# Infini-attention block with a gated FFN: sums evicted from PSUM bank by bank, full-width transposes, and a newly planned order

## Chip, cores and metric

The kernel runs on one core of a Trainium2 chip. The metric is the device time of one execution in microseconds (us). Engines are named as in the profile: PE (TensorE), DVE (VectorE), ACT (ScalarE), POOL (GpSimd), SP (the queue that issues most DMAs).

## What is computed

The input is 2048 tokens of width 448 in bfloat16. A layer norm with scale and shift from a condition vector `c` comes first, then attention with a compressive memory, then a second modulated layer norm and a gated FFN. The core of the reference:

```python
for s in range(4):                       # segments of 512 tokens, 16 heads of 28
    logits = einsum('bhqd,bhkd->bhqk', qs, ks) * scale + mask
    a_dot = softmax(logits) @ vs
    pq = phi(qs)                         # phi(t) = t + 1 if t > 0 else exp(t)
    a_mem = (pq @ M) / (pq . z + 1e-06)
    outs.append(g * a_mem + (1 - g) * a_dot)
    M = M + phi(ks)^T @ vs;  z = z + sum(phi(ks))
x = x + ga * (concat(outs) @ wo)
h = layernorm(x) * (1 + cb) + sb
x = x + gb * ((sigmoid(h @ w_gate) * (h @ w_up)) @ w_down)
```

The six vectors `sa, ca, ga, sb, cb, gb` are `silu(c) @ w_mod`; `q, k, v` come from the first modulated layer norm; the FFN's inner width is 1792.

## The kernel before

The work is cut into four segments of 512 tokens. For each segment the kernel does a layer norm (`ln1`), turns the tokens over so that features lie on partitions (`hT`), projects q, k and v (`proj`), computes logits, exps and attention sums for four groups of four heads (`attention`, `unit`), updates the memory (`memory`), does the output projection and second layer norm (`wo_ln2`), and the FFN in 14 chunks of 128 inner features (`ffn`).

Nothing is issued in the order of these loops. Every piece of work is a node of a graph (`Graph.add`) with a duration, the engines that may do it, its inputs, the ring slots it takes and the slots it uses. When all nodes are made, `Graph.run` plays the graph through on planned clocks: at each moment, an engine that is free takes the ready node with the highest rank (longest path to the end) plus priority. The priorities are the tables `PRM`, one entry a node. `STAY` is a bonus for a PE node in the same array mode as the one before it. Where two engines may do a node, `COST` weighs their planned durations against each other. The order found is the order in which the instructions are issued on each engine, SP's loads included; the durations in the code have no other effect. A slot is given back when the plan says that its last user has ended.

All matmul results lie in one PSUM tile `ps` of eight banks; a node takes banks by number as they are free, and any two free banks may make a pair. Transposes also write to PSUM.

The places that the change touches:

- `proj` (lines 891 to 923). A job of 14 matmuls at line 903 makes the k sums and the q sums of four heads in two banks. One eviction (`evac`, line 886 on ACT or line 888 on DVE) reads both banks with one access, whose step is the distance of the banks, and writes k and q with one access into the joint tile `kq_t`, in which the slots of k come first and those of q after them. The v sums of two token tiles (line 916) leave in the same way into two neighbouring tiles of `vt`. Planned durations are 840 and 1130 ns (ACT, DVE) for k and q, and 760 and 1010 for v.
- `pf2`, `lesser`, `greater` make the access on two banks:

```python
i, j = lesser(a, b), greater(a, b)
return ps[:, i:j + 1:j - i, :]
```

- `turned_once` (line 777) turns one token tile over in four transposes (line 782) for the second layer norm of every segment and the first layer norm of the last one. The tile `xn` has 512 columns, of which the last 64 are zeros, set once (line 585). The fourth transpose reads only 64 columns.
- `turned` (line 831) does the same for the other first layer norms with eight transposes a tile, at line 841, two of which are 64 wide. Each of the two then modulates the result into `hT` on DVE or ACT (lines 861, 863 and 797, 795).
- `memory` (line 940): transposes of k (line 950), exps, matmuls of the memory (line 969).
- Other lines that are named below: 1011 logits, 1025 and 1031 exps, 1041 and 1038 masks, 1070 attention sums, 1140 output projection, 1162 FFN gate and up, 1181 FFN down, 622 and 635 layer norm.

Of the kernel before, what the change touches and what calls it, by code (L numbers as in the profile page):

```python
# [7 lines left out]
BF16 = mybir.dt.bfloat16  # L8
# [43 lines left out]
    "mask": (3126070, 2037934, 2803786, 3505785, 3188009, 2852632, 3303572, 3533526, 3992806, 2545585, 2629448,  # L52
# [16 lines left out]
    "mem": (-123901, -236157, 540966, -358460, -167904, 74719, 3507, 330720, 598584, 648670, 613158, -673453, -487145,  # L69
# [18 lines left out]
    "tanh": (1212395, 1541798, 840180, 1390091, 2102771, 1519654, 1567471, 1153766, 1921369, 2277244, 2695092,  # L88
# [17 lines left out]
        -778556, -813758, 65300, -841338, -1381324, -626743, -443000, -615156, -409610, -941217, -462304, -867816,  # L106
        -636982, -465394, 452513, -909815, -380427, -10400),
}
STAY = 145391
COST = {"ACT": 0.829, "DVE": 0.85, "POOL": 0.804}  # L110


# [1127 lines left out]
```

## Time and profile before

| | |
|---|---|
| three runs, median (lowest, highest) | 268.8 us (268.68, 271.85) |
| profiled execution, time | 269.32 us |
| profiled execution, span | 267.6 us |
| busy PE, DVE, ACT, POOL | 248.3, 194.3, 162.2, 31.3 us |
| moved by DMA | 15.58 MB |

The span goes from the first to the last instruction in the profile, and the time has 1.7 us around it. Busy time is the union of an engine's instructions; a matmul's end is modelled, and matmuls overlap, so that the mean length of one (377 ns) is longer than the distance to the next. A row of the timeline or of the groups names the engine, the line of the kernel, what is written and read, and the count; a bracket or the part behind the bar tells how long the engine stood idle before it and which instruction ended that.

### The profile page before, as it was taken

The page shows a single profiled execution, that of the slowest core. Times are in us where ns is not written, and L with a number is a line of the kernel's source. Part 1 is how long each engine was busy: PE and PEld are TensorE (multiplying, and loading weights), DVE is VectorE, ACT ScalarE, POOL GpSimd, SP SyncE. Part 2 cuts the span into 40 slices and gives each one's busy share as a digit, 9 for nine tenths or more (in the row PEclk, how much of TensorE's full clock was granted, in tenths as well). Part 3 has the DMA queues.
Part 4 walks back from the last instruction along what each step waited for, and adds up shares of the span by engine and source line. Part 5 has one row for each costly group of instructions (what it writes and reads, how often), then busy time and mean ns, then how long its engine had stood idle before and what let it go on. Part 6 is the DMA issues. An engine that isn't in the chain of part 4 may idle for free.

```text
span 267.6 us, 6070 instructions
## 1 busy us (share of the span) xinstructions
PE 248.3 (93%) x2518; PEld 115.2 (43%) x2518; DVE 194.3 (73%) x440; ACT 162.2 (61%) x174; POOL 31.3 (12%) x82
## 2 busy tenths in 40 slices
PE   8977588788999999998999999989999999999994
PEld 3623334444455444444445333443444444434442
DVE  4793596999979999999799869357789735243331
ACT  5057586999866789748798786376970232223210
POOL 6113031000610000014010013200001300000000
PEclk9999999999999999999999999999999999999999
DMA  6999999500020000030300000003000003000011
GB/s 163 233 214 226 216 202 225 185 4 2 1 62 12 0 2 2 0 83 23 85 22 2 2 0 4 0 0 105 17 4 17 2 0 86 20 0 21 17 34 34
DMA packets 12423, 15.58 MB, mean 58 GB/s; under 512 B 939, under 2 KB 10860, under 8 KB 12396
## 3 DMA queue, kind: packets, MB, share of 16 engines
q1 hardware_dynamic: 11868, 14.57, 23.9%
q10 hardware_dynamic: 528, 0.63, 0.9%
q8 instruction: 19, 0.31, 0.5%
q14 instruction: 8, 0.07, 0.1%
HBM read 11.07 MB, written 1.84 MB: 48 GB/s over the span
## 4 chain that ended last, share of the span: by engine, by line
PE 58%; DVE 17%; DMA 16%; ACT 5%; issue 1%; SPq 1%; ACTq 0%; DVEq 0%
PE ps L1162 27%; PE ps L1181 15%; DMA wgu<-in_B_w_up_dram 5%; DMA x_sb<-in_A_x_dram 4%; DMA fT<-in_w_mod_dram 4%; PE ps L782 3%; DMA pT<-in_w_mod_dram 3%; DVE st L622 2%; PE ps L1140 2%; PE ps L1011 2%; PE ps L916 2%; ACT pT L1025 2%; PE ps L1070 2%; PE ps L903 2%; DVE pT L1041 2%; DVE fT L1169 2%
## 5 line engine op out<-in xcount | busy, mean ns | idle before, releaser
L1162 PE MATMUL ps<-hT,wgu 64*128 64x512 bf16 x784 | 92.6, 377 | 0.4 <-DVE fT L1169 0.3
L1167 ACT ACTIVATE tt<-ps 128x512 f32<-128x512 f32 x56 | 33.5, 598 | 52.6 <-PE ps L1162 52.3
L1025 ACT ACTIVATE pT<-ps 128x2048 bf16<-128x2048 f32 x32 | 60.1, 1878 | 7.1 <-PE ps L1011 7.1
L1162 PEld LDWEIGHTS <-wgu 64*128 64x128 bf16 x784 | 38.9, 94 | 46.4 <-issue 10.3
L1169 DVE SCALAR_TENSOR_TENSOR fT<-tt,ps 128x512 bf16<-128x512 f32 x56 | 37.9, 681 | 27.6 <-ACT tt L1167 27.5
L1181 PE MATMUL ps<-wd_sb,fT 128*128 128x448 bf16 x224 | 47.0, 354 | 0.8 <-ACT kT L886 0.8
L903 PE MATMUL ps<-hT,wqk 64*128 64x512 bf16 x224 | 28.4, 377 | 4.2 <-ACT kT L886 2.7
L1181 PEld LDWEIGHTS <-fT 128*128 128x128 bf16 x224 | 19.9, 98 | 23.7 <-issue 7.6
L629 POOL TENSOR_SCALAR rs<-mv 128x1 f32<-128x1 f32 (+1 forms) x29 | 6.7, 230 | 162.0 <-DVE mv L623 136.1
L1041 DVE TENSOR_TENSOR pT<-pT,cmask 128x512 bf16<-128x512 bf16 x55 | 21.1, 412 | 5.8 <-ACT pT L1025 4.7
L622 DVE BATCH_NORM_STATS2 st<-x_sb 128x6 f32<-128x448 bf16 x32 | 19.7, 615 | 3.1 <-DMA x_sb<-in_A_x_dram 2.6
L886 ACT CAST kT<-ps 128x1024 bf16<-128x1024 f32 x14 | 14.1, 1012 | 9.6 <-PE ps L903 5.7
L903 PEld LDWEIGHTS <-wqk 64*128 64x128 bf16 x224 | 11.4, 94 | 17.5 <-issue 6.7
L630 POOL TENSOR_TENSOR rs<-rs,mhalf 128x1 f32<-128x1 f32 (+1 forms) x29 | 17.2, 593 | 2.4
L1031 ACT ACTIVATE pT<-ps 128x2048 bf16<-128x2048 f32 x8 | 15.0, 1878 | 2.9 <-PE ps L1011 2.8
L1011 PE MATMUL ps<-kT 28*128 28x512 bf16 (+3 forms) x256 | 16.0, 300 | 0.2
L1188 DVE TENSOR_TENSOR ot<-ps,x_sb 128x448 bf16<-128x448 f32 x16 | 9.8, 616 | 8.1 <-PE ps L1181 7.9
L1070 PE MATMUL ps<-pT,vt 128*32 128x512 bf16 (+3 forms) x256 | 11.4, 301 | 3.1 <-ACT vt L886 1.0
L1140 PE MATMUL ps<-wo_sb,oT 128*128 128x448 bf16 x64 | 13.3, 353 | 0.6 <-ACT kT L886 0.6
L916 PE MATMUL ps<-wvv,hT 64*128 64x448 bf16 x112 | 11.8, 350 | 1.4 <-DVE kT L888 1.4
L635 DVE TENSOR_SCALAR xn<-x_sb,mv,rs 128x448 bf16<-128x448 bf16 x32 | 11.2, 387 | 1.9 <-POOL rs L630 1.9
L1102 DVE STREAM_TRANSPOSE A<-aT 128x512 uint32<-128x512 uint32 (+1 forms) x16 | 10.1, 637 | 1.8 <-ACT aT L1094 1.6
(101 smaller groups left out, 239.9 us busy)
## 6 DMA issues: line engine op xcount, KB each, us to landing
out_dram<-ot SPq DMA_DIRECT2D x16, 112.0 KB, 1.7
wgu<-in_B_w_gate_dram SPq DMA_DIRECT2D x3, 448.0 KB, 13.3
wgu<-in_B_w_up_dram SPq DMA_DIRECT2D x3, 448.0 KB, 14.2
hT<-hT SPq DMA_DIRECT2D x5, 256.0 KB, 3.2
hT<-hT SPq DMA_DIRECT2D x5, 192.0 KB
x_sb<-in_A_x_dram SPq DMA_DIRECT2D x2, 448.0 KB
wd_sb<-in_B_w_down_dram SPq DMA_DIRECT2D x2, 448.0 KB, 11.4
wvv<-in_A_wv_dram SPq DMA_DIRECT2D x2, 392.0 KB, 7.2
```

What stands on the lines that cost most here:

```text
L622: nc.vector.bn_stats(st_r[:, st.at, :], src)
L630: nc.gpsimd.tensor_tensor(r, r, mhalf[:, 0:w], ALU.pow)
L903: nc.tensor.matmul(ps[:, b, :], lhsT=w, rhs=piece(hT, i, half), start=(i == 0), stop=(i == NP - 1))
L916: nc.tensor.matmul(ps[:, b, 0:D], lhsT=piece(hT, i, half)[:, (t + half) * P:(t + half + 1) * P], rhs=wvv[half * HR:(half + 1) * HR, chunk_ ...
L1011: nc.tensor.matmul(ps[:, lg.at + hs, o:o + nq], lhsT=kT_r[r, k.at, hcs[u], kb * P:(kb + 1) * P], rhs=qT_r[r, q.at, hcs[u], kb * P:L], star ...
L1025: nc.scalar.activation(pT_r[:, pTs[units[0]].at, :, w0:w0 + L], ps_, AF.Exp, scale=scale)
L1041: nc.vector.tensor_tensor(blk, blk, cmask[:].rearrange("p (o k) -> p o k", o=1).to_broadcast([P, 4, P]), ALU.mult)
L1140: nc.tensor.matmul(pf(b)[:, 0:D], lhsT=oT_r[:, oT.at, k, t * P:(t + 1) * P], rhs=wo_sb[:, k, :], start=(k == 0), stop=(k == NHC - 1))
L1162: nc.tensor.matmul(pf(b), lhsT=wgu[half * HR:(half + 1) * HR, chunk_of(i, half), fs], rhs=piece(hT, i, half), start=(i == 0), stop=(i == N ...
L1167: a = act(485, lambda gp=gp, tt=tt: nc.scalar.activation(tt_r[:, tt.at, :], pf(gp), AF.Tanh, scale=0.5), [n], use=[gp, tt], prio=pr("tanh" ...
L1169: f = dve(597, lambda up=up, tt=tt, ft=ft: nc.vector.scalar_tensor_tensor(fT_r[:, ft.at, :], tt_r[:, tt.at, :], 1.0, pf(up), op0=ALU.add, ...
L1181: nc.tensor.matmul(pf(b)[:, 0:D], lhsT=fT_r[:, fts[fc].at, t * P:(t + 1) * P], rhs=wd_sb[:, fc, :], start=(fc == 0), stop=(fc == NFC - 1))
```

## The change

Four things are changed.

- The pair accesses are gone. k and q are evicted by one instruction each, from one bank into a tile of its own (`kT`, `qT`), and each of the two v sums by one instruction. Work that needs k alone now depends on k's eviction alone. Planned durations are 475 and 600 ns (ACT, DVE) for k and q, and 420 and 540 for v.
- `turned_once` turns all four chunks over with 128 columns, the zeros included, and depends on the nodes that set the zeros.
- Some planned durations are other numbers.
- All tables of `PRM`, and `STAY` and `COST`, are new, and so the order on every engine, and which engine does what may go to two.

```diff
-STAY = 145391
-COST = {"ACT": 0.829, "DVE": 0.85, "POOL": 0.804}
+STAY = 117564
+COST = {"ACT": 0.769, "DVE": 1.026, "POOL": 0.838}
...
-    def pf2(a, b):
-
-        i, j = lesser(a, b), greater(a, b)
-        return ps[:, i:j + 1:j - i, :]
...
-    kq_t = ring("kT", NKT, [P, NHC, L], BF16, NQ)
-    kT_r, qT_r = kq_t[:, 0:NKT], kq_t[:, NKT:NKT + NQ]
-    G.pool("qT", NQ)
+    qT_r = ring("qT", NQ, [P, NHC, L], BF16)
+    kT_r = ring("kT", NKT, [P, NHC, L], BF16)
...
-                w, c = P if kc < NK - 1 else HR, (kc % 2) * L + t * P
-                nc.tensor.transpose(pb(bs[kc // 2])[0:w, c:c + P], xn_r[:, xn.at, kc * P:kc * P + w], ident[:])
-        return add("PE", 4 * 57, fn, [n, n_ident, prev], ...
+                c = (kc % 2) * L + t * P
+                nc.tensor.transpose(pb(bs[kc // 2])[:, c:c + P], xn_r[:, xn.at, kc * P:(kc + 1) * P], ident[:])
+        return add("PE", 4 * 57, fn, [n, n_ident, *n_xpads, prev], ...
...
-                for half, b in ((0, greater(bk, bq)), (1, lesser(bk, bq))):
+                for half, b in ((0, bq), (1, bk)):
...
-            k_n[(s, hc)] = q_n[(s, hc)] = evac(
-                lambda hc=hc: kq_t[:, k.at:NKT + q.at + 1:NKT + q.at - k.at, hc, :], lambda bq=bq, bk=bk: pf2(bk, bq), [n],
-                [bk, bq, k, q], pr("ev", s), (840, 1130))
+            k_n[(s, hc)] = evac(lambda hc=hc: kT_r[:, k.at, hc, :], lambda bk=bk: pf(bk), [n], [bk, k], pr("ev", s))
+            q_n[(s, hc)] = evac(lambda hc=hc: qT_r[:, q.at, hc, :], lambda bq=bq: pf(bq), [n], [bq, q], pr("ev", s))
...
-            v_n[(s, t)] = v_n[(s, t + 1)] = evac(
-                lambda t=t: vt_r[:, v.at, t:t + 2, :, 0:Dh],
-                lambda b2=b2: pf2(*b2)[:, :, 0:D].rearrange("p t (h d) -> p t h d", d=Dh), [n, *n_vpad, *n_vone], [*b2, v],
-                pr("ev", s), (760, 1010))
+            for i, b in enumerate(b2):
+                v_n[(s, t + i)] = evac(
+                    lambda t=t + i: vt_r[:, v.at, t, :, 0:Dh],
+                    lambda b=b: pf(b)[:, 0:D].rearrange("p (h d) -> p h d", d=Dh), [n, *n_vpad, *n_vone], [b, v], pr("ev", s),
+                    (420, 540))
```

The planned durations that differ are those of the casts of `wqk` on DVE (300 to 400 ns), the coefficients (1600 to 1900), the transposes of `turned` (456 a node to 617 by token tile, or to 456, 700, 456 and 228 by chunk), the features of k (1100 to 1140) and the memory's matmuls (960 to 500).

More of the change, by code (lines that the diff above doesn't have):

```diff
@@ L26 @@
 PRM = {
[25 rows of a table removed]
-    "mask": (3126070, 2037934, 2803786, 3505785, 3188009, 2852632, 3303572, 3533526, 3992806, 2545585, 2629448,
[16 rows of a table removed]
-    "mem": (-123901, -236157, 540966, -358460, -167904, 74719, 3507, 330720, 598584, 648670, 613158, -673453, -487145,
[18 rows of a table removed]
-    "tanh": (1212395, 1541798, 840180, 1390091, 2102771, 1519654, 1567471, 1153766, 1921369, 2277244, 2695092,
[16 rows of a table removed]
-    "phi": (-799224, -246641, 907400, 58712, 713795, 293729, 48058, -771610, 598455, 1007813, -442110, -145510,
-        -778556, -813758, 65300, -841338, -1381324, -626743, -443000, -615156, -409610, -941217, -462304, -867816,
-        -636982, -465394, 452513, -909815, -380427, -10400),
-}
-STAY = 145391
-COST = {"ACT": 0.829, "DVE": 0.85, "POOL": 0.804}
[26 rows of a table added]
+    "mask": (963858, 878708, 235739, 1223611, 1391530, -102597, -104966, 472822, 258034, 1200420, 909156, 512615,
[16 rows of a table added]
+    "mem": (-1298360, -1504223, -1263515, -642432, -1965746, -1960682, -731404, -1074059, -2252320, -1855358,
[18 rows of a table added]
+    "tanh": (-1094092, -896048, -228471, -624919, -316181, 197126, -464105, -9529, 253670, 553043, 888654, -418483,
[16 rows of a table added]
+    "phi": (-94060, -446182, 761668, -133799, -234099, -552907, 224741, -223919, -440733, 111372, -1637638, 218500,
+        -1001211, 187206, 480416, 1057063, -230293, 510690, 415024, 49114, 656808, -60207, -446109, -470855, -95918,
+        -1378409, -26144, -1462738, -286576, -49681),
+}
+STAY = 117564
+COST = {"ACT": 0.769, "DVE": 1.026, "POOL": 0.838}
 class Slot:
@@ L411, in pb, with ring @@
         return ps[:, s.at, :].bitcast(BF16)
-    def lesser(a, b):
-        return min(a.at, b.at)
-    def greater(a, b):
-        return max(a.at, b.at)
-    def pf2(a, b):
-        i, j = lesser(a, b), greater(a, b)
-        return ps[:, i:j + 1:j - i, :]
-    def ring(name, n, shape, dtype, more=0):
+    def ring(name, n, shape, dtype):
         G.pool(name, n)
-        return const.tile([shape[0], n + more, *shape[1:]], dtype, name=name)
+        return const.tile([shape[0], n, *shape[1:]], dtype, name=name)
     def steps(a, *dims):
@@ L711, in pad @@
                     vec(e).tensor_copy(dst, src)
-            W_p.append(add(("DVE", "ACT", "POOL"), (300, 838, 830), pad, [W_qk[half], n_pads, n_th, *ln0], prio=BIG if h else 2.5 * BIG, lock=True))
+            W_p.append(add(("DVE", "ACT", "POOL"), (400, 838, 830), pad, [W_qk[half], n_pads, n_th, *ln0], prio=BIG if h else 2.5 * BIG, lock=True))
     b_w = bank()
@@ L760, in coef_fn @@
         nc.vector.tensor_reduce(rmask[:], rsel[:], axis=mybir.AxisListType.X, op=ALU.add)
-    n_coef = dve(1600, coef_fn, [n_cf, n_hsel], lock=True)
+    n_coef = dve(1900, coef_fn, [n_cf, n_hsel], lock=True)
     ga_mm, n_ga = mod_rep(2, 0, 1.0)
@@ L780, in fn @@
             for kc in range(NK):
-                w, c = P if kc < NK - 1 else HR, (kc % 2) * L + t * P
-                nc.tensor.transpose(pb(bs[kc // 2])[0:w, c:c + P], xn_r[:, xn.at, kc * P:kc * P + w], ident[:])
-        return add("PE", 4 * 57, fn, [n, n_ident, prev], take=[*bs, hT] if t == 0 else (), use=[xn] if t == 0 else [*bs, hT, xn],
+                c = (kc % 2) * L + t * P
+                nc.tensor.transpose(pb(bs[kc // 2])[:, c:c + P], xn_r[:, xn.at, kc * P:(kc + 1) * P], ident[:])
+        return add("PE", 4 * 57, fn, [n, n_ident, *n_xpads, prev], take=[*bs, hT] if t == 0 else (), use=[xn] if t == 0 else [*bs, hT, xn],
                    prio=prio, mode="F")
@@ L845, in turned @@
             for t in range(TPS):
-                n = add("PE", 8 * 57, lambda t=t: [tr(t, i) for i in range(NP)], [ns[t][0], n_ident, n],
+                n = add("PE", 617, lambda t=t: [tr(t, i) for i in range(NP)], [ns[t][0], n_ident, n],
                         take=[*bs, hT] if t == 0 else (), use=[ns[t][1]] if t == 0 else [*bs, ns[t][1]], prio=prio(),
@@ L851, in turned @@
             for j in range(NK):
-                done.append(add("PE", 8 * 57, lambda j=j: [tr(t, i) for i in range(2 * j, min(2 * j + 2, NP)) for t in range(TPS)],
+                done.append(add("PE", (456, 700, 456, 228)[j], lambda j=j: [tr(t, i) for i in range(2 * j, min(2 * j + 2, NP)) for t in range(TPS)],
                                 [n for n, _ in ns] + done[-1:], take=[bs[j]] if j else [bs[j], hT],
@@ L900, in mm @@
             def mm(i, hc=hc, bq=bq, bk=bk):
-                for half, b in ((0, greater(bk, bq)), (1, lesser(bk, bq))):
+                for half, b in ((0, bq), (1, bk)):
                     w = wqk[half * HR:(half + 1) * HR, chunk_of(i, half), hc * 4:(hc + 1) * 4, :].rearrange("p h e -> p (h e)")
-                    nc.tensor.matmul(ps[:, b, :], lhsT=w, rhs=piece(hT, i, half), start=(i == 0), stop=(i == NP - 1))
+                    nc.tensor.matmul(pf(b), lhsT=w, rhs=piece(hT, i, half), start=(i == 0), stop=(i == NP - 1))
             n = job(lambda: pr("pj", s), hn, [*W_p[2 * hc:2 * hc + 2], prev if s or hc > 2 else None], mm,
@@ L914, in mm @@
             def mm(i, t=t, b2=b2):
-                for half, b in enumerate((lesser(*b2), greater(*b2))):
-                    nc.tensor.matmul(ps[:, b, 0:D], lhsT=piece(hT, i, half)[:, (t + half) * P:(t + half + 1) * P],
+                for half, b in enumerate(b2):
+                    nc.tensor.matmul(pf(b)[:, 0:D], lhsT=piece(hT, i, half)[:, (t + half) * P:(t + half + 1) * P],
                                      rhs=wvv[half * HR:(half + 1) * HR, chunk_of(i, half), :], start=(i == 0),
@@ L957, in memory @@
                     use=[e], prio=pr("mem", s), lock=True)
-            made.append(dve(1100, lambda b=b, e=e, pk=pk: nc.vector.scalar_tensor_tensor(
+            made.append(dve(1140, lambda b=b, e=e, pk=pk: nc.vector.scalar_tensor_tensor(
                 pk_r[:, pk.at].rearrange("p u t k -> p (u t k)"), pb(b), 1.0, e_r[:, e.at, 0, :], op0=ALU.add, op1=ALU.max),
@@ L971, in mm @@
                                          stop=(kb == TPS - 1), tile_position=(0, HP * hs), skip_group_check=True)
-        m = add("PE", NHC * 240, mm, made + [v_n[(s, t)] for t in range(TPS)], take=[b], use=[*pks, vt_of[s]], mode="C",
+        m = add("PE", 500, mm, made + [v_n[(s, t)] for t in range(TPS)], take=[b], use=[*pks, vt_of[s]], mode="C",
                 prio=pr("mem", s))
```

151 rows, old and new, of the table PRM are left out of this document.

## The prediction

> **What bounds the kernel now.** I read the page's busy shares and slices first, then its chain, then the busy times by stretch, then the groups with their waits, and last the timeline at the places where the waits lie.
>
> ```profile
> span 267.6 us, 6070 instructions
> ...
> PE 248.3 (93%) x2518; PEld 115.2 (43%) x2518; DVE 194.3 (73%) x440; ACT 162.2 (61%) x174; POOL 31.3 (12%) x82
> ...
> PE   8977588788999999998999999989999999999994
> ...
> PE 58%; DVE 17%; DMA 16%; ACT 5%; issue 1%; SPq 1%; ACTq 0%; DVEq 0%
> ```
>
> PE carries the end of the kernel, but the first ten slices (6.7 us each) do not look like the rest: all but one are at 5 to 8 tenths. The same by stretch (busy us of each engine; the first FFN matmul starts at 77.65, so I cut there):
>
> ```profile
> 0.00:14.40 14.40, 12.60 (x125) 6.88 (x125) 9.25 (x35) 4.07 (x13) 5.25 (x23) 1.00 0.89 198
> 14.40:77.60 63.20, 51.37 (x647) 26.05 (x647) 50.73 (x131) 49.93 (x42) 12.57 (x29) 1.00 0.62 132
> 77.60:267.60 190.00, 184.35 (x1751) 82.32 (x1746) 134.30 (x276) 108.19 (x120) 13.46 (x30) 1.00 0.08 23
> ...
> 50.00:60.00 10.00, 7.74 (x114) 4.54 (x112) 9.90 (x21) 9.67 (x9) 0.00 (x0) 1.00 0.06 18
> ...
> 80.00:90.00 10.00, 10.00 (x102) 4.65 (x100) 9.76 (x19) 7.34 (x11) 0.00 (x0) 1.00 0.07 15
> ...
> 77.65 0.59 PE L1162 MATMUL ps<-hT,wgu 64*128 64x512 bf16 x4
> ```
>
> From 14.4 to 77.6 PE stands idle for 63.20 - 51.37 = 11.8 us; in the 190 us after it for only 5.65 us, the last few of them after the last matmul. So the time can fall in two ways: less idle PE before 77.6, or less PE work after it.
>
> **What the paired evictions do now.** The groups, with mean ns and what ended the idle time before them:
>
> ```profile
> L1025 ACT ACTIVATE pT<-ps 128x2048 bf16<-128x2048 f32 x32 | 60.1, 1878 | 7.1 <-PE ps L1011 7.1
> L1181 PE MATMUL ps<-wd_sb,fT 128*128 128x448 bf16 x224 | 47.0, 354 | 0.8 <-ACT kT L886 0.8
> L903 PE MATMUL ps<-hT,wqk 64*128 64x512 bf16 x224 | 28.4, 377 | 4.2 <-ACT kT L886 2.7 <-ACT vt L886 1.0 <-ACT hT L863 0.4
> L886 ACT CAST kT<-ps 128x1024 bf16<-128x1024 f32 x14 | 14.1, 1012 | 9.6 <-PE ps L903 5.7 <-PE ps L916 2.8 <-PE ps L1070 1.0
> L1140 PE MATMUL ps<-wo_sb,oT 128*128 128x448 bf16 x64 | 13.3, 353 | 0.6 <-ACT kT L886 0.6
> L916 PE MATMUL ps<-wvv,hT 64*128 64x448 bf16 x112 | 11.8, 350 | 1.4 <-DVE kT L888 1.4
> L1070 PE MATMUL ps<-pT,vt 128*32 128x512 bf16 x64 | 6.4, 388 | 3.1 <-ACT vt L886 1.0 <-DVE hT L861 0.9 <-ACT kT L886 0.8
> L841 PE MATMUL ps<-ident,xn 128*128 128x128 bf16 x72 | 5.9, 220 | 2.3 <-ACT vt L886 1.6 <-DVE vt L888 0.7
> L886 ACT CAST vt<-ps 128x896 bf16<-128x896 f32 x6 | 5.4, 906 | 6.3 <-PE ps L916 3.5 <-PE ps L903 2.8
> L888 DVE CAST kT<-ps 128x1024 bf16<-128x1024 f32 x2 | 2.4, 1224 | 4.3 <-ACT pT L1025 4.3
> L888 DVE CAST vt<-ps 128x896 bf16<-128x896 f32 x2 | 2.2, 1079 | 0.0
> ```
>
> Two things stand out. The k and q sums come from line 903, yet their eviction also waits for the v sums of line 916 (2.8 us), for attention sums of line 1070 (1.0) and, on DVE, for an exp of line 1025 (4.3); the v sums come from 916, yet their eviction waits for 903 (2.8). No data of theirs goes through those instructions. And PE waits for an eviction in 2.7 + 1.0 + 1.4 + 1.0 + 0.8 + 1.6 + 0.7 + 0.8 + 0.6 = 10.6 us, partly ahead of work that has nothing to do with it (down projection, output projection). My reading: an access that names two banks with a step is kept apart from everything that touches the banks between them. The timeline fits:
>
> ```profile
> 25.34 1.88 ACT L1025 ACTIVATE pT<-ps 128x2048 bf16<-128x2048 f32 x1 [0.82 <-PE ps L1011]
> ...
> 27.23 1.22 DVE L888 CAST kT<-ps 128x1024 bf16<-128x1024 f32 x1 [3.73 <-ACT pT L1025]
> ...
> 28.50 1.50 PE L916 MATMUL ps<-wvv,hT 64*128 64x448 bf16 x14 [1.39 <-DVE kT L888]
> ...
> 29.69 0.25 DVE L585 MEMSET xn<- 128x32 uint32 x5
> ...
> 30.04 1.01 ACT L886 CAST kT<-ps 128x1024 bf16<-128x1024 f32 x1 [2.83 <-PE ps L916]
> ...
> 31.91 1.18 PE L841 MATMUL ps<-ident,xn 128*128 128x128 bf16 x20 [1.58 <-ACT vt L886]
> ```
>
> Exp, then an eviction, then matmuls, then an eviction, then transposes: five steps on three engines, one behind the other, though each engine had work. The late cases are two:
>
> ```profile
> 122.41 2.00 PE L903 MATMUL ps<-hT,wqk 64*128 64x512 bf16 x14
> ...
> 124.34 0.73 PE L1070 MATMUL ps<-pT,vt 128*32 128x512 bf16 x16
> ...
> 125.12 1.01 ACT L886 CAST kT<-ps 128x1024 bf16<-128x1024 f32 x1 [0.71 <-PE ps L1070]
> ...
> 126.18 1.11 PE L1181 MATMUL ps<-wd_sb,fT 128*128 128x448 bf16 x5 [0.79 <-ACT kT L886]
> ...
> 175.95 1.27 PE L1070 MATMUL ps<-pT,vt 128*32 128x512 bf16 x32 [1.00 <-ACT vt L886]
> ```
>
> **Part 1, single evictions: cost.** 24 pairs (14 + 6 on ACT, 2 + 2 on DVE) become 48. ACT: from 1024 to 2048 elements it goes from 1012 to 1878 ns, 0.846 ns an element, so 512 elements are about 1012 - 433 = 579 ns and 448 about 906 - 379 = 527; two of them cost 146 and 148 ns more than the pair. Twenty pairs: 2.9 us. On DVE (1224 - 1079) / 128 = 1.13 ns an element gives 644 and 571 ns, 64 ns more for a pair, 0.26 us for four. This lies beside PE. In 14.4 to 77.6, where 12 of the ACT pairs stand, ACT rises from 49.93 to 51.7 busy. The first bank of a pair is free after 579 ns in place of 1012, the second after 1158, or 644 if the two engines share them. Logits need both k and q: 16 x 0.146 = 2.3 us of later starts at worst, behind which exps queue on ACT; the exp of the group before covers it where ACT is busy. The Trainium skill, "Perfetto Trace Analysis", section "Optimizing Scalar/DVE Operations", speaks against this part: each ACT instruction on PSUM has an access overhead of some 51 ns and grouping helps a saturated engine; by that figure twenty more would be an estimated 1.0 us, against my 2.9 from rows.
>
> **Part 1: gain.** Late: 0.79 + 1.00 = 1.8 us of PE idle, against an otherwise full PE; I take 1.5. Early: the other 8.8 us. Some of them are plain waits for a bank that stay. And the stretch cannot shrink at will: ACT and DVE must do 51.7 and 51.0 us of work in it, and in 50 to 60 they already run at 9.67 and 9.90 of 10. If it shrinks by 5 us to 58.2, they are at 89% and 88%. By 9 us they would be at 95%. Bounds 0 and 8.8; I take 5.
>
> **Part 2, full width.** Line 782 turns four chunks per tile, the fourth 64 columns wide. Now all are 128 wide (the columns behind 448 are zeros).
>
> ```profile
> 73.80 0.62 PE L950 MATMUL ps<-ident,kT 128*128 128x128 bf16 x8
> ...
> 74.54 1.84 PE L782 MATMUL ps<-ident,xn 128*128 128x128 bf16 x16
> ...
> 104.95 1.06 PE L950 MATMUL ps<-ident,kT 128*128 128x128 bf16 x16
> ...
> L782 PE MATMUL ps<-ident,xn x80: 217/219/243, 74.5 to 221.7; 128*128 128x128 bf16 x60, 128*64 128x128 bf16 x20
> ```
>
> Sixteen in a row take 1.84 us with every fourth one narrow, 1.06 us where all are full: 0.78 us per 16, and 80 make 3.9 us, nearly all behind 74 us, where PE is the bound. The lower bound is the narrow ones' own excess, 20 x (243 - 217) ns = 0.5 us. I take 3.5, near the like-for-like rows, as DVE at 9.76 of 10 (80 to 90) may take some back. The Trainium skill, "TensorEngine Tiling (Array Packing)", section "Key Properties", says that a change of tiling mode drains TensorE; the trace agrees as far as 1.84 against 1.06 goes, and by that rule the whole 3.9 would go. The new wait on the zeroed columns costs nothing: the memsets ran at 29.69, the first of these transposes at 74.54. The evictions behind them keep their rows.
>
> **Part 3, tiles of their own and the new order.** Separate q and k tiles move no work. Durations and weights only steer the order in which the same instructions and DMAs are issued, on all queues (SP's loads among them). What a new order is worth no row can say: at best it takes the whole 11.8 us of early idle, at worst it makes an engine late that is not. I put 0, between these, since the plan now also sees shorter transposes and no hidden links.
>
> **Sum**, against the profiled execution's 269.32 us (its span is 267.6): 269.3 - 5 - 1.5 - 3.5 - 0 = 259.3. The median of the three times, 268.8, lies 0.5 below the profiled one, so I forecast **258.8**, with 255.5 to 262.5 for this case. A measurement of this kernel tells about 2% from no change, so below 263.4 is faster and above 274.2 slower.
>
> **Rivals.** (A) *FFN work moves forward.* With ACT no longer stopped behind stray links, attention of the first segment ends sooner and FFN matmuls fill the early PE idle whole: 268.8 - 11.8 - 1.5 - 3.5 = 252.0; half of the rest beyond my 5 gives 255.4. For it: loads are done by 50 us (DMA share 0.06 in 50 to 60). Against: DVE is full from 50 on, and the first segment's layer norm goes through it. I give it 253.5.
>
> (B) *The early waits are replaced.* The chain runs on DVE from 47 to 72 us, these being its first and last pieces there:
>
> ```profile
> 47.56 0.36 DVE xn L635
> ...
> 71.29 0.52 DVE st L622
> ```
>
> If that stretch keeps its length, or if the links were real bank reuse and stay with single banks, the early gain is about 1.5, the late 0.5, and DVE takes back part of the transposes (2 left): 268.8 - 4 = 264.8, within 262.5 to 268.8.
>
> (C) *ACT becomes the gate, and the time is longer.* The new weights make DVE dearer (0.85 to 1.026) and ACT cheaper (0.829 to 0.769), so work that may go to either goes to ACT, which also has every exp.
>
> ```profile
> L861 DVE TENSOR_SCALAR hT<-ps,cols 128x512 bf16<-128x512 bf16 x16 | 7.9, 534 | 2.8 <-PE ps L841 2.7
> ...
> L863 ACT ACTIVATE hT<-ps,cols 128x512 bf16<-128x512 bf16 x5 | 3.8, 776 | 5.4 <-DVE hT L861 5.3
> ```
>
> If all 16 of line 861 moved at 776 ns (12.4 us) and the four DVE pairs as singles (2 x 1158 + 2 x 1054 ns = 4.4), with the 1.8 of part 1 ACT would have 49.9 + 18.6 = 68.5 us of work before 77.6; at the 0.967 of 50 to 60 that is 70.9 us, 7.7 longer. Less 5 of the other parts: 271.5. It decides once more than 63.2 x 0.967 - 49.9 = 11.2 us are added to ACT. Against it: the plan counts ACT's time too.
>
> **Chances.** Forecast 0.52, A 0.15, B 0.26, C 0.07 (of it 0.04 over 274.2). About 0.05 of B lies below 263.4. Faster 0.52 + 0.15 + 0.05 = 0.72, same 0.24, slower 0.04. The range 252 to 267 leaves out about 0.04 of A, 0.07 of B and all of C, 0.18 together.
>
> **What would show it.** Right: evictions of 579 and 527 ns on ACT with no wait on another line's sums; PE's waits for lines 886 and 888 under 3 us; sixteen transposes of line 782 in about 1.06 us; first FFN matmul near 72. B shows as a first FFN matmul still near 77 with PE waiting for exps or layer norm; A as one before 68; C as ACT over 95% before it. Wrong altogether: PE idle after the first FFN matmul well over 6 us, from an order that leaves PE waiting on DVE in the second half.

## The result

The changed kernel took 259.85 us (median of 4 runs, 257.97 to 260.27) against 270.33 for the kernel before (4 runs): a ratio of 0.962 with a 95% interval of 0.952 to 0.972. The forecast was 258.8 in a range of 252 to 267. Executions more than 1.5% above the fastest of the same kernel (one of `a_narrow`, below, took 477.69 us) count in the medians, but not in the ratios.

The page of the changed kernel (its own time 260.27 us):

```profile
span 258.5 us, 6138 instructions
...
PE 245.3 (95%) x2530; PEld 116.1 (45%) x2530; DVE 195.2 (76%) x441; ACT 161.0 (62%) x188; POOL 37.9 (15%) x91
...
PE   8599969999998899999999999999999999999994
...
PE 69%; DVE 15%; DMA 8%; ACT 4%; issue 2%; SPq 1%; DVEq 0%
```

PE is idle for 258.5 - 245.3 = 13.2 us in place of 19.3, and busy for 3.0 us less: together the 9.1 us that the span lost. Among the first 14 slices 5 are at 8 tenths or less (8, 5, 6, 8, 8) in place of 9. By stretch (busy us of PE, its weight loads, DVE, ACT and POOL, then the granted clock), cut where before was cut and where the first FFN matmul now stands:

```profile
14.40:77.60 63.20, 59.04 (x788) 29.57 (x786) 57.04 (x146) 52.60 (x58) 18.52 (x37) 0.98 0.64 141
...
83.00:258.50 175.50, 170.90 (x1598) 77.27 (x1590) 124.95 (x255) 98.42 (x111) 14.14 (x31) 1.00 0.08 22
```

From 14.4 to 77.6 PE is idle for 4.2 us in place of 11.8. The evictions on ACT and what PE waits for (the lines have moved: 875 and 877 are the old 886 and 888, 892 the old 903, 904 the old 916, 1059 the old 1070, 771 the old 782, 731 the old 742, which reads beta; 1068, the old 1079, evicts attention sums on DVE):

```profile
L875 ACT CAST kT<-ps 128x512 bf16<-128x512 f32 x13 | 7.7, 590 | 4.0 <-PE ps L892 4.0
L875 ACT CAST qT<-ps 128x512 bf16<-128x512 f32 x10 | 5.9, 586 | 4.0 <-PE ps L892 4.0
L875 ACT CAST vt<-ps 128x448 bf16<-128x448 f32 x10 | 5.1, 534 | 0.8 <-PE ps L904 0.7
...
PE ps L892 <- DVE aT L1068: 1.7, 1, 1.7
PE ps L731 <- DMA beta_row<-in_A_beta_dram: 1.6, 1, 1.6
...
PE ps L1059 <- ACT qT L875: 0.3, 1, 0.3
...
PE ps L904 <- DVE vt L877: 0.2, 1, 0.2
...
78.39 1.07 PE L771 MATMUL ps<-ident,xn 128*128 128x128 bf16 x16
```

Each of these evictions waits for its own line's sums only (so do those on DVE), PE waits for evictions in 0.5 us in place of 10.6, and sixteen full-width transposes take 1.07 us in place of 1.84.

### The profile page after: what moved, and what is told of

Its sections match the earlier page's. It is cut to its first block, busy times and chain, and to the rows that moved or that the text cites. A ratio compares the mean times of both kernels' runs of the same rounds, so it can differ in the third digit from the quotient of the medians.

```text
span 258.5 us, 6138 instructions
## 1 busy us (share of the span) xinstructions
PE 245.3 (95%) x2530; PEld 116.1 (45%) x2530; DVE 195.2 (76%) x441; ACT 161.0 (62%) x188; POOL 37.9 (15%) x91
## 3 DMA queue, kind: packets, MB, share of 16 engines
HBM read 11.07 MB, written 1.84 MB: 50 GB/s over the span
## 4 chain that ended last, share of the span: by engine, by line
PE 69%; DVE 15%; DMA 8%; ACT 4%; issue 2%; SPq 1%; DVEq 0%
PE ps L1151 33%; PE ps L1170 16%; DMA x_sb<-in_A_x_dram 5%; PE ps L892 5%; PE ps L1129 4%; DMA beta_row<-in_A_beta_dram 3%; PE ps L1000 3%; PE ps L1059 2%; DVE pT L1030 2%; PE ps L904 2%; ACT pT L1014 1%; DVE pk L947 1%; PE ps L830 1%; PE ps L1195 1%; DVE st L611 1%
## 5 line engine op out<-in xcount | busy, mean ns | idle before, releaser
L1151 PE MATMUL ps<-hT,wgu 64*128 64x512 bf16 x784 | 90.1, 377 | 0.0
L1170 PE MATMUL ps<-wd_sb,fT 128*128 128x448 bf16 x224 | 46.3, 353 | 0.0
L1030 DVE TENSOR_TENSOR pT<-pT,cmask 128x512 bf16<-128x512 bf16 x49 | 19.1, 419 | 7.7 <-ACT pT L1014 5.4
L1027 POOL TENSOR_SCALAR_AFFINE_SELECT pT<-pT 128x512 bf16<-128x512 bf16 x15 | 9.5, 638 | 94.1 <-DVE x_sb L1132 43.7
L1000 PE MATMUL ps<-qT,kT 28*128 28x512 bf16 (+3 forms) x256 | 15.9, 301 | 0.6 <-ACT hT L784 0.6
L1059 PE MATMUL ps<-pT,vt 128*32 128x512 bf16 (+3 forms) x256 | 11.8, 302 | 1.2 <-DVE x_sb L1132 0.6
L1000 PEld LDWEIGHTS <-kT 28*128 28x128 bf16 x256 | 4.5, 92 | 15.0 <-issue 14.8
## 6 DMA issues: line engine op xcount, KB each, us to landing
wgu<-in_B_w_gate_dram SPq DMA_DIRECT2D x3, 448.0 KB, 11.6
```

Source lines behind the costliest of these rows:

```text
L1000: nc.tensor.matmul(ps[:, lg.at + hs, o:o + nq], lhsT=kT_r[r, k.at, hcs[u], kb * P:(kb + 1) * P], rhs=qT_r[r, q.at, hcs[u], kb * P:L], star ...
L1030: nc.vector.tensor_tensor(blk, blk, cmask[:].rearrange("p (o k) -> p o k", o=1).to_broadcast([P, 4, P]), ALU.mult)
L1151: nc.tensor.matmul(pf(b), lhsT=wgu[half * HR:(half + 1) * HR, chunk_of(i, half), fs], rhs=piece(hT, i, half), start=(i == 0), stop=(i == N ...
L1170: nc.tensor.matmul(pf(b)[:, 0:D], lhsT=fT_r[:, fts[fc].at, t * P:(t + 1) * P], rhs=wd_sb[:, fc, :], start=(fc == 0), stop=(fc == NFC - 1))
```

## The experiments

The theory was that the two edits make the gain: a pair with a step is tied to the banks between its two, and a narrow transpose costs PE. The chief rivals were that the waits are for banks that would be short anyway, and that the new order makes the gain. The plan is a search, so any edit of its graph gives another order. Most experiments therefore keep a planned order as it is and edit only what a node issues.

**The two edits apart and together, in the old order; the second undone in the new.** `b_full`, whose plan keeps its old nodes:

```diff
-                w, c = P if kc < NK - 1 else HR, (kc % 2) * L + t * P
-                nc.tensor.transpose(pb(bs[kc // 2])[0:w, c:c + P], xn_r[:, xn.at, kc * P:kc * P + w], ident[:])
+                c = (kc % 2) * L + t * P
+                nc.tensor.transpose(pb(bs[kc // 2])[:, c:c + P], xn_r[:, xn.at, kc * P:(kc + 1) * P], ident[:])
```

> The kernel before, in its own order, with one change: line 782 turns all four chunks over with 128 columns. Theory (a narrow transpose among wide ones costs PE): sixteen in a row take about 1.06 us in place of 1.84, and the time falls by 2.5 to 3.9 us, to a ratio of 0.986 to 0.991. Rival (DVE, at 9.8 of 10 while these run, takes it back): the transposes get shorter all the same, but the time falls by less than 1 us.

`b_split`, whose node stays one node with its planned duration and engine:

```diff
-            if e == "ACT":
-                nc.scalar.copy(dst(), src())
...
+            d, s = dst(), src()
+            one = [(d[:, h], s[:, h]) for h in range(2)] if True else [(d, s)]
+            for d, s in one:
+                if e == "ACT":
+                    nc.scalar.copy(d, s)
...
```

On DVE it is done likewise.

> The kernel before, in its own order and with its own engine for each eviction, but each pair is evicted by two instructions, one per bank, one right behind the other. Theory (a pair with a step is tied to the banks between): evictions no longer wait for sums of other lines, PE's waits for lines 886 and 888 fall from 10.6 to under 4 us, and the time falls by 4 to 6.5 us (ratio 0.976 to 0.985) although ACT is busy 2.9 us longer. Rival (the waits were for the banks themselves, or the order makes the gain): the waits stay at 9 us or more and the time is unchanged or up to 2 us longer.

`b_both` has both diffs; `a_narrow` is the changed kernel with the first diff reversed.

> Both edits together, still in the order of the kernel before: so what is left between this and the changed kernel is the new order with the new choice of engines. Theory (the two edits make the gain): 6.5 to 10 us below the kernel before, ratio 0.963 to 0.976. Rival (the order makes it): not more than 4 us below, so that the new order is worth 6 us or more.

> The changed kernel with the fourth chunk of its transposes at 64 columns again, all else as changed. Theory (narrow transposes cost PE 3.9 us, and PE is the bound after 83 us): 2.5 to 3.9 us above the changed kernel, ratio to the kernel before about 0.971 to 0.976. Rival (hidden behind DVE): under 1 us above it, ratio at most 0.966.

Measured, as ratios to the kernel before (269.57 us in these runs):

| kernel | ratio (95%) | us, median |
|---|---|---|
| `b_full` | 0.992 (0.989 to 0.996) | 267.32 |
| `b_split` | 0.962 (0.957 to 0.967) | 258.83 |
| `b_both` | 0.955 (0.950 to 0.960) | 256.83 |
| `a_narrow` | 0.974 (0.971 to 0.977) | 262.90 |

Splitting alone, in an unchanged order, gives 0.038 x 269.57 = 10.2 us, as much as the whole change, and more than the 6.5 at most that was expected. `b_both` gained more than expected for the same reason. The page and the groups of `b_split` (889 is its eviction on ACT, 906 and 919 make the sums, 1165 is FFN gate and up):

```profile
PE 247.2 (96%) x2518; PEld 113.8 (44%) x2518; DVE 194.1 (76%) x444; ACT 162.8 (63%) x194; POOL 31.2 (12%) x82
...
14.40:77.60 63.20, 58.74 (x731) 29.47 (x731) 58.76 (x150) 55.42 (x64) 12.56 (x29) 1.00 0.67 139
...
L889 ACT CAST kT<-ps 128x512 bf16<-128x512 f32 x28 | 15.0, 597 | 2.9 <-PE ps L906 2.7
L889 ACT CAST vt<-ps 128x448 bf16<-128x448 f32 x12 | 5.8, 535 | 4.1 <-PE ps L919 4.0
...
L1165 PE MATMUL ps<-hT,wgu x784: 372/376/387, 69.0 to 244.4; 64*128 64x512 bf16 x196
```

PE's idle time falls from 19.3 to 256.9 - 247.2 = 9.7 us, and the first FFN matmul comes at 69.0 in place of 77.7, with the same instructions in the same order before it. The place that the prediction showed at 25 to 32 us now reads:

```profile
22.13 1.88 ACT L1028 ACTIVATE pT<-ps 128x2048 bf16<-128x2048 f32 x1
22.44 1.29 DVE L891 CAST kT<-ps 128x512 bf16<-128x512 f32 x2 [0.59 <-PE ps L906]
...
23.75 1.52 PE L919 MATMUL ps<-wvv,hT 64*128 64x448 bf16 x14
...
25.52 1.96 PE L841 MATMUL ps<-ident,xn 128*128 128x128 bf16 x32
```

The exp and the eviction on DVE run side by side (before, the eviction started after the exp's end), and from the exp's start to the transposes it takes 3.4 us, where it took 6.6. Two evictions in a row overlap, as two rows of the same view show:

```profile
23.95 1.07 ACT L889 CAST kT<-ps 128x512 bf16<-128x512 f32 x2
...
25.27 0.97 ACT L889 CAST vt<-ps 128x448 bf16<-128x448 f32 x2 [0.24 <-PE ps L919]
```

Each of the two lasts 597 or 535 ns, but both together occupy ACT for 1.07 or 0.97 us, against 1.01 and 0.91 for the pair access: some 0.06 us more.

Of the full width, the transposes and the page of `b_full`:

```profile
PE 244.5 (92%) x2518; PEld 113.6 (43%) x2518; DVE 194.2 (73%) x440; ACT 162.2 (61%) x174; POOL 31.3 (12%) x82
...
74.46 1.05 PE L782 MATMUL ps<-ident,xn 128*128 128x128 bf16 x16
```

PE works 248.3 - 244.5 = 3.8 us less, as the rows had it (3.9), but the time falls by 0.0076 x 269.57 = 2.0 us (1.1 to 3.0), between what the theory (2.5 to 3.9) and the rival (under 1) expected: in the profile PE's idle time grows by 1.2 to 20.5. In the new order the edit is worth 0.974 - 0.962 = 0.012, 3.3 us, from two sets of runs and thus roughly; against the changed kernel's second ratio below, 0.967, it would be 1.9.

**Which banks are tied.** In the old order 18 of the 24 pairs have at least one bank between them, and 6 are neighbours. `b_split_far` splits only the 18, `b_split_near` only the 6:

```diff
+            one = [(d[:, h], s[:, h]) for h in range(2)] if max(x.at for x in use[0:2]) - min(x.at for x in use[0:2]) > 1 else [(d, s)]
```

In `b_split_near` the line ends on `== 1 else [(d, s)]`.

> The kernel before in its own order, in which only those 18 of the 24 pairs are evicted bank by bank whose banks have at least one bank between them (most are two apart); the 6 pairs of neighbouring banks leave by one instruction as before. Theory (the tie is to the banks between): the whole gain of splitting all 24, ratio 0.959 to 0.967. Rival (the gain comes from shorter evictions, which free each bank sooner): three quarters of it, ratio 0.970 to 0.974.

> The complement: only the 6 pairs of neighbouring banks are evicted bank by bank, the other 18 by one instruction with a step. Theory (the tie is to the banks between, and neighbours have none): no gain, ratio 0.996 to 1.003. Rival (shorter evictions free banks sooner): a quarter of the gain, ratio 0.988 to 0.992.

Far: 0.961 (0.954 to 0.968). Near: 0.997 (0.993 to 1.001). The whole gain is with the pairs that have banks between. First three groups of the near one, where the split evictions stand beside pairs with a step, then one of the far one:

```profile
L889 ACT CAST kT<-ps 128x1024 bf16<-128x1024 f32 x10 | 10.0, 1015 | 8.5 <-PE ps L906 4.6 <-PE ps L919 2.8 <-PE ps L1073 0.7
...
L889 ACT CAST kT<-ps 128x512 bf16<-128x512 f32 x8 | 4.3, 592 | 1.1 <-PE ps L906 1.1
L891 DVE CAST kT<-ps 128x1024 bf16<-128x1024 f32 x2 | 2.5, 1226 | 4.3 <-ACT pT L1028 4.3
```

```profile
L889 ACT CAST kT<-ps 128x1024 bf16<-128x1024 f32 x4 | 4.0, 1011 | 1.8 <-PE ps L906 1.8
```

The pairs with a step still wait for 919, 1073 and an exp; single banks and pairs of neighbours wait only for the line that makes their sums. So it isn't the length of an eviction, nor that it frees its bank sooner. Nor is it the other thing that a pair writes with a step, the joint tile of k and q: the lines waited for (919, 1073, 1028) touch none of it, and in `b_split_far` the neighbouring pairs of k and q still write it with one access and wait for 906 alone. The Trainium skill, "PSUM — Partial Sum Buffer", section "PSUM bank collisions raise a hardware error", says that two engines may not touch one bank at a time, reads against reads included. That tells why an eviction on DVE is put in line with an exp on ACT at all; the runs show that the line was drawn through banks which the pair didn't touch. No run here shows a collision.

**The order.** `b_both` beat the changed kernel, which has the same two edits, the new order, and tiles of their own for k and q (no run tests these alone; where the text says "new order", they are part of it). Both were run again on one chip, with a third, `a_oldprm`: the changed kernel's code with the old `PRM`, `STAY` and `COST`.

> The changed kernel once more, on one chip and in turns with the next two, to size the new order. Theory (the order's worth is 0 or negative): 0.957 to 0.965 of the kernel before, 1 to 3 us above the old order with both edits. Rival (the earlier difference was chance): the two within 1 us.

> Old order with both edits, once more. Theory (the new order gives a little back): ratio 0.949 to 0.956, 1 to 3 us under the changed kernel. Rival: within 1 us of it.

> The changed kernel's code and planned durations (single evictions as work of their own, full width) but with the priorities, STAY and COST of the kernel before, each pair's priority given to both its evictions; the order is planned anew from them. Theory (the priorities fit only the graph they were made for): it loses against both others, 260 to 266 us, ratio 0.964 to 0.985. Rival (the edits carry the gain under any sensible order): within 2 us of the changed kernel, ratio 0.952 to 0.966.

Against 271.21 us for the kernel before: the changed kernel 0.967 (0.961 to 0.973, 260.91 us), `b_both` 0.952 (0.947 to 0.957, 256.79), `a_oldprm` 1.030 (1.024 to 1.035, 277.17). Here the new order costs 0.015 x 271.2 = 4.0 us (1.9 to 6.1, the two intervals combined); in the first sets of runs it was 0.962 - 0.955 = 0.007, 1.8 us, within the noise. Part of it is the granted clock of PE: where an execution's mean granted clock is 0.998 or more, the changed kernel took 257.97 and 258.56 us, and `b_both` 255.63 to 257.61 (8 executions, median 256.4), some 1.9 us less, roughly, as the changed kernel has only two such. The rest of the 4 us lies in executions at a lower clock, 8 of 10 of the changed kernel's and 2 of 10 of `b_both`'s. The old priorities, planned anew with the edits as nodes, lose more than both edits bring, and more than either expectation allowed (266 us at most):

```profile
span 273.3 us, 6171 instructions
...
PE 255.0 (93%) x2556; PEld 116.5 (43%) x2556; DVE 196.3 (72%) x446; ACT 161.4 (59%) x190; POOL 32.6 (12%) x84
...
PE ps L709 <- ACT pT L952: 2.0, 1, 2.0
PE ps L830 <- DVE pk L885: 1.4, 1, 1.4
```

No eviction is on top of its waits. So a table of priorities fits the one graph that it was searched for, and it is the emitted order of before, not its table, that carries over.

**Where the new order may lose.** First the changed kernel's start, and below it the same place in `b_both`:

```profile
13.00:16.00 3.00, 3.00 (x69) 2.37 (x67) 1.54 (x6) 0.84 (x1) 0.00 (x0) 0.50 1.13 232
...
10.19 0.16 PE L731 MATMUL ps<-beta_row,ones 1*128 1x16 bf16 x1 [1.64 <-DMA beta_row<-in_A_beta_dram]
...
15.26 2.78 PE L1195 MATMUL ps<-ident 128*128 128x512 bf16 x7
...
17.97 1.25 PE L892 MATMUL ps<-hT,wqk 64*128 64x512 bf16 x10
```

```profile
14.15 1.48 PE L906 MATMUL ps<-hT,wqk 64*128 64x512 bf16 x6
```

PE waits for 32 bytes of beta, the granted clock is 0.50 from 13 to 16 us, and seven matmuls that only fill a gap take 2.78 us. The first projection is 3.8 us later. But that holds for this pair of profiles alone: in the second ones (`after5` and `b_both5`), where the clock from 13 to 16 us is 1.00 in the changed kernel, the first projections start at 15.34 and 15.22 us. `a_beta` and `b_both_beta` issue beta's load third on SP's queue, and nothing else is moved:

```diff
+        c, beta = self.early
+        order.remove(beta)
+        order.insert(order.index(c) + 1, beta)
```

> The changed kernel in its own order, but the 32-byte load of beta is issued third on SP's queue, ahead of the large load that it stood behind. In the changed kernel PE waits 1.64 us for it at 10.2 us, the granted clock is 0.50 from 13 to 16 us, and the first projection starts at 17.97 us against 14.15 with the old order and both edits. Theory (the new order loses at its start): PE starts projections 1.5 to 3.5 us earlier, the clock stays at 1, and the time falls by as much, ratio 0.949 to 0.956. Rival (the loss lies elsewhere in the order): under 1 us, ratio 0.958 or more.

> Old order with both edits, and beta's load issued third on SP's queue. There PE waited 1.46 us for it at 8.4 us, ahead of the first transposes. Theory (the start is on the path of every later step): 0.7 to 1.5 us less, ratio 0.949 to 0.953. Rival (the first layer norm, done on DVE at 9.6 us, holds the last transposes anyway): no change, ratio 0.954 to 0.957.

`a_beta`: 0.958 (0.953 to 0.962, 258.70 us); `b_both_beta`: 0.951 (0.946 to 0.955, 257.02 us). The second is not told apart from its parent: its ratio is in the theory's range, but PE waits for the layer norm instead, as the rival had it. The first is not told apart from the changed kernel's 0.962 and lies 2.5 us below its 0.967. At a full clock there is no gain: three executions took 258.19 to 258.90 us, against 257.97 and 258.56. Its projections start at 15.1, close to the 15.34 of `after5`. One of its four executions has a lower clock; whether the move made that rarer is not shown. Another wait showed in the second profile of the changed kernel (`after5`):

```profile
33.41 0.63 DVE L611 BATCH_NORM_STATS2 st<-x_sb 128x6 f32<-128x448 bf16 x1 [1.43 <-DMA x_sb<-in_A_x_dram]
...
35.69 3.17 PE L892 MATMUL ps<-hT,wqk 64*128 64x512 bf16 x14 [3.17 <-DVE aT L1068]
...
30.00:35.00 5.00, 2.14 (x50) 1.53 (x47) 2.50 (x9) 5.00 (x5) 1.60 (x3) 0.94 1.04 185
35.00:40.00 5.00, 4.31 (x17) 1.28 (x16) 3.70 (x11) 0.81 (x2) 3.20 (x8) 0.50 1.04 218
```

DVE stands before statistics of x tiles that haven't landed; behind them stands the eviction that frees PE's bank. `a_beta_aev` puts that eviction ahead of them:

```diff
+        order.remove(aev)
+        order.insert(order.index(pv) + 1, aev)
```

> The changed kernel with beta's load early, and in addition the first attention unit's eviction (line 1068) moved on DVE from behind the layer-norm statistics of four x tiles to ahead of them. In the changed kernel PE stands before a projection at 36 us until this eviction has freed its bank, 1.75 us in one profile and 3.17 us in another, in which the statistics also waited 1.43 us for x. Theory (this place of the new order is most of its loss): PE's wait there falls under 0.9 us and the time to 0.949 to 0.955 of the kernel before. Rival (the next wait takes its place): the wait moves elsewhere, ratio 0.957 or more.

0.957 (0.952 to 0.961, 258.96 us): no gain over `a_beta`. PE's wait there fell to 1.0 us, and the rival's number came out; its executions at a full clock took 258.07 to 258.24 us. So no single place of the new order that was tried explains its loss at a full clock. What does stays open; the changed kernel issues 19 filling matmuls where the old order has 7.

The version that beats both kernels is `b_both`: 256.8 us, 0.955 and 0.952 of the kernel before in two sets of runs.

## Why the prediction was right, and where it was not

The time came out 1 us from the forecast, but so close by luck: part 1 brought 3.7 us more than was taken for it, part 2 1.5 us less, and the order, put at 0, cost some 2 to 4 us.

- **Part 1, mechanism: right and shown.** The stray waits were read off the groups, and splitting only the pairs with banks between them removes the waits and brings the whole gain.
- **Part 1, size: too small.** I took 5 + 1.5 of at most 10.6 us; it is 10.2 (8.9 to 11.6). The step that failed is the cap: I stopped where ACT and DVE would be at 89% and 88% of a stretch shortened by 5 us. In `b_split` the stretch from 14.4 us to the first FFN matmul is 54.6 us long, 8.6 shorter; ACT is busy for 49.31 us of it (90%) and DVE for 50.30 (92%). So the 9.67 and 9.90 of 10 us from 50 to 60 were no sign of a ceiling for the stretch.
- **Cost of single evictions: lengths nearly right, cost too high.** 597 and 535 ns in place of 579 and 527. But the sum of two lengths is not what two in a row take: they overlap, and a pair costs some 60 ns more of ACT, not 146 and 148. All evictions on ACT take 15.0 + 5.8 = 20.8 us in place of 14.1 + 5.4 = 19.5, so 1.3 more, where 2.9 were added; the prediction's other estimate, 1.0, was nearer. It stays beside PE.
- **Part 2: work right, worth too large.** PE's work fell by 3.8 us (3.9 predicted); 2.0 us of it reached the time in the old order, 3.5 were taken. That waits take some back was named, but undersized.
- **Part 3: wrong.** The order was put at 0 "since the plan now also sees shorter transposes and no hidden links"; it costs 4.0 us (1.9 to 6.1) in the runs side by side, and some 1.9 of these at a full clock.
- **Signs to watch for.** "First FFN matmul near 72" failed: it is at 83.1. The new order puts more of the other work ahead of the FFN (all 112 matmuls of line 904 stand before 83 us), so this moment compares nothing between two orders; between kernels of one order it does (77.7 and 69.0).
- **Rivals.** A's early FFN nearly came, but with the old order (69.0 in `b_split`, 68.4 in `b_both`, before 68 for A), and not with A's time. B fell by `b_split`: the stretch gets shorter, and the links go with single banks. C did not occur: ACT is busy for 52.60 of 63.20 us. The rival of the experiments, an order that makes the gain, has the sign wrong.

## What to carry to other kernels

When an instruction waits for work that neither makes its data nor uses its banks, look at what its access names: one with a step over a shared tile may be ordered against everything in between, and two plain accesses, some 0.06 us dearer for a pair, brought 10 us here. The lengths of instructions that follow each other may overlap: take what two occupy from a timeline before adding them up. Test an edit in the emitted order first, since a new plan brings gains and losses of its own of several us, and priorities don't carry over to another graph. Before a wait is called the loss of an order, look for it in a second profile, and at each execution's clock. A total that comes out right says nothing of its terms until each has been run alone.

## What was not expected of the hardware

The granted clock of PE fell to 0.50 for some us early in some runs: at 13 to 16 us in the changed kernel's first profile and at 35 to 40 in its second, after a stretch in which PE was busy for 2.14 of 5 us. Its four first executions had spans of 258.5, 256.3, 258.5 and 257.8 us at mean clocks of 0.987, 1.0, 0.987 and 0.993, so one such fall costs some 2 us (an estimate from these four). A small wait early in the kernel may then cost more than its length; that a wait of PE brings the fall is not shown. The Trainium skill, "TensorE: Matmul & The Clock Gate", section "What's actually happening", tells of a monitor that halves the clock after an idle window of about 3.4 us; the trace agrees in the half, and the 3.17 us wait is near that window, but no run here measures it. Moving beta's load, or the eviction behind it, did not settle it: of six executions of `a_beta_aev` one again had 0.986 and two had 0.993.
